# Linear attention and gated FFN in fp32 precision: product groups summed onto ScalarE's copies in PSUM, both parts of x in DRAM, and the first pass's outputs by Strassen's scheme

## The chip, the cores and the metric

The kernel runs on one core of one Trainium2 chip. The metric is the device time of one execution in microseconds (us); the median of several runs is given. One more execution was recorded by the hardware profiler, and every statement on single instructions comes from it. Engines: PE is TensorE's matmuls and PEld its weight loads, DVE is VectorE, ACT is ScalarE, POOL is GpSimd, SP is SyncE, which issues most of the DMAs.

## The reference

```python
def _attn_ref(q, k, v, w_phi):                       # q, k, v: 8 x 8 heads x 576 x 64
    def phi(x):
        proj = np.einsum('bhsd,df->bhsf', x, w_phi)  # 128 features
        proj = proj - np.max(np.abs(proj), axis=-1, keepdims=True)
        return np.concatenate([np.exp(proj), np.exp(-proj)], axis=-1)
    q_p, k_p = (phi(q), phi(k))
    kv = np.einsum('bhsf,bhsd->bhfd', k_p, v)
    z = np.sum(k_p, axis=2)
    num = np.einsum('bhsf,bhfd->bhsd', q_p, kv)
    den = np.einsum('bhsf,bhf->bhs', q_p, z)[..., None] + 1e-06
    return num / den

def _moe_ref(x, w_gate, w_val, w_out):               # x: 4608 tokens x 512, d_ff = 1536
    gate = 1.0 / (1.0 + np.exp(-(x @ w_gate)))
    val = x @ w_val
    return gate * val @ w_out
```

The result of the attention, with its heads side by side, is the x of the FFN. All is in fp32.

## The kernel before

**Precision.** A product of two fp32 matrices is made of three matmuls. Each operand is split into a high part, rounded to the type that TensorE multiplies at full speed (`fp32r`), and a low part, which is the rest. A product is high x high + high x low + low x high. The high part is a copy on ScalarE (CAST), the low part a subtraction on VectorE.

**Layout.** Features or hidden units lie on the 128 partitions and tokens along a row; `out` is 512 x 4608, feature by token. The hidden layer has 12 blocks of 128 units.

**Phase A** (about the first 600 us) does the attention in 32 steps (8 batches x 4 pairs of heads, `attend`), which write x to `xscr` in DRAM. Between these steps it does the first four hidden blocks of the FFN for chunks of 512 tokens: `load_x` (L900) brings a chunk of x and splits it, L925 multiplies gate and value, L982 the outputs, and the sum of the four blocks goes to `yscr` in DRAM (L1011).

**Phase B** does the other eight blocks, in four pairs of blocks, by Strassen's scheme: a product of 2 x 2 blocks is made of 7 products of combined blocks, not 8. One such product is called a *group* here (`group`). Its inputs are the seven weight combinations of a pair (made by `combine` from gate, value or output weights, each in a high and a low part) and seven blocks of x named 11, 21, 22, T1 to T4 (made by `x_blocks`). A group has 7 products; each is 6 matmuls of 128 x 384 (two steps of depth by three parts). In L1286 each product gets a PSUM bank, and VectorE adds the banks up (L1305) into buffers in SBUF, after ScalarE has copied the first one there (L1311): one copy and five additions a group. The results are four quarters: two feature halves by two halves of 384 tokens.

Phase B goes twice over the six chunks of 768 tokens, which are called turns here:

- In the *first pass* (`first_pass`), `x_blocks` loads four blocks of x, combines and splits all seven (ScalarE L1213, VectorE L1217), and stores T1 to T4 in `tscr`. Then come four groups (gate and value of pairs 0 and 1). The hidden halves are split, and the outputs are ordinary matmuls (L1407, 96 a turn). `finish` loads what phase A left in `yscr` (L1161), adds it (L1168) and writes `out` (L1172). Beside it, one combination of weights for the second pass is made in each turn.
- In the *second pass*, T1 to T4 come from `tscr`, the blocks 11, 21 and 22 from `xscr` and are split again. Four groups (pairs 2 and 3) are followed by two groups for the outputs (`sent`), each over both pairs. Their results are copied or added into SBUF and added to `out` by DMAs that GpSimd issues (L1516, accumulating). The last turn adds `out` itself, before it writes it.

**What sets the order.** Nothing is issued in the order of the source. Each operation is recorded with its engine, an assumed duration, what it reads and writes and a rank; `Plan.run` then walks through time and takes for each engine, of what could start within a short window (`NEAR`), the operation of lowest rank. For DMAs it assumes one wire with a rate (`RATE`) and a landing time. Buffers come from rings, which may share memory (`arena`, `r_f`, `r_y`, ...): whoever takes a slot waits for its last user. Each engine executes its list strictly in the order found so.

Of the kernel before, what the change touches and what calls it, by code (L numbers as in the profile page):

```python
# [20 lines left out]
P = 128  # L21
# [18 lines left out]
RB = 70 << 10  # L40
FB = 15 << 10
# [18 lines left out]
KEEP = 30.0  # L60
SPAN = 46.0
PASS = 43.8

# [87 lines left out]
class Plan:  # L151
# [5 lines left out]
    RATE = 0.26, 0.36  # L157

# [22 lines left out]
    def run(self):  # L181
        free = dict.fromkeys(self.NEAR, 0.0)
        ready = {e: [] for e in free}
        mode, wire, rate = None, 0.0, self.RATE[0]
# [30 lines left out]
        while left:  # L215
            best = None
            for e, cs in ready.items():
                ts = [(t, o) for o in cs if (t := start(o)) is not None]
                if not ts:
                    continue  # L220
                first = min(t for t, _ in ts) + self.NEAR[e]
# [18 lines left out]
            if o.eng in ("SP", "POOL"):  # L240
                wire = max(wire, t) + o.lag / rate * 1e-6
                end = wire + 2.0
# [4 lines left out]
            if o.opens:  # L247
                rate = self.RATE[1]
# [23 lines left out]
def attention_moe(  # L272
# [54 lines left out]
    for hd in range(2):  # L327
# [4 lines left out]
    xscr = [dram.tile([P, NC4, CW], F32, tag=f"xs{c}", name=f"xs{c}") for c in range(NCH)]  # L332
    yscr = [dram.tile([P, NC4, CW], F32, tag=f"ys{c}", name=f"ys{c}") for c in range(NCH)]
    tscr = [dram.tile([8, P, DC], F32, tag=f"t{c}", name=f"t{c}") for c in range(NDC)]
    wscr = [dram.tile([2, P, DM], F32, tag=f"wo{j}", name=f"wo{j}") for j in range(JA + 4)]
# [3 lines left out]
        for m in range(3)  # L339
    }  # L340
# [6 lines left out]
    third = arena("three", "third", FB, F32R)  # L347
# [12 lines left out]
    r_y1 = x.ring(3, DM)  # L360
    r_h = x.ring(8, 2 * HT)
    r_wo = x.ring(8, DM)
    r_hA = low(48).ring(4, 4 * HT)
    r_hB = low(42).ring(1, 3 * HT) + third().ring(3, 3 * HT)
    r_O = low(72).ring(2, 7 * 2 * P)
    x = high()
    r_G = x.ring(8, 7 * 2 * P)
    r_stage = x.ring(2, 7 * 2 * P)
    r_O += r_stage
    r_swo = high(56).ring(7, DM)  # L370
    r_x7 = high(42).ring(2 * NC4, CW)
    r_f = flat().ring(5, HT) + flat(12).ring(6, HT)
    r_tmp = flat(21).ring(3, 2 * HT)
    r_f2 = r_f[:5] + flat(8).ring(2, HT) + r_f[8:10]
    r_T = flat(12).ring(1, 3 * HT)
    r_V = flat(19.5).ring(2, 4 * HT)
    x = more()
    r_raw2, r_top2 = x.ring(2, 2 * DM, U32), x.ring(1, DM, U32)
    r_sum = x.ring(1, 2 * DM)
# [15 lines left out]
    def dve(n, fn, reads, writes, rank, k=1.0, after=()):  # L395
        return plan.op("DVE", 0.07 + n / 960 / k, 0.16, fn, reads, writes, rank, after=after)
# [18 lines left out]
    xmark = [Buf() for _ in range(NCH)]  # L415
    ymark = [Buf() for _ in range(NCH)]
    closing, opening, feeding, exps = [], [], [], []

    def attend(i):
# [346 lines left out]
        if b == 0:  # L766
# [9 lines left out]
            )  # L776
        t = 0
        while t < S:
# [4 lines left out]
                lambda c=c, o=o, t=t, wd=wd: nc.sync.dma_start(  # L783
                    xscr[c][:, p, o : o + wd], xp()[:, t : t + wd]
# [109 lines left out]
    def load_x(c, r, rings, after=()):  # L894
        for p in range(NP):
# [4 lines left out]
                lambda p=p, xl=xl: nc.sync.dma_start(xl().bitcast(F32), xscr[c % NCH][:, p, :]),  # L900
# [12 lines left out]
            )  # L913

# [71 lines left out]
    def first_js(c, r, step):  # L986
# [5 lines left out]
        for t in range(NC4):  # L992
            acc, y = Buf(banks, [P, CW]), Buf([r_y], [P, CW])

            def go(t=t, acc=acc):
# [15 lines left out]
                256 << 10, lambda t=t, y=y: nc.sync.dma_start(yscr[c][:, t, :], y()),  # L1011
# [39 lines left out]
    last.opens = [a().cells for a in (high, more)]  # L1051
# [15 lines left out]
    def combine(n, m, r, rings, after):  # L1067
# [7 lines left out]
        for i, j in enumerate(pair(n)):  # L1075
# [4 lines left out]
            dve(  # L1080
# [6 lines left out]
            )  # L1087
        p12, p21 = (1, 2) if m < 2 else (2, 1)
# [24 lines left out]
        combined.append(plan.ops[-1])  # L1113
# [24 lines left out]
    def out_weight(j, r, rings, after):  # L1138
        wh, wl = Buf(rings, [P, DM]), Buf(rings, [P, DM])
        weigh(j, 2, r, False, wh, wl, slice(0, DM), None, after, True)  # L1140
        return wh, wl

    def pieces(dc, h):

        t, e, s = dc * DC + h * HT, dc * DC + h * HT + HT, 0
        while t < e:
            c, o = divmod(t, CW)
            wd = min(CW - o, e - t)
            yield c, o, s, wd
            t, s = t + wd, s + wd  # L1150

    def final(m, dc, h):
        return out[m * P : m * P + P, dc * DC + h * HT : dc * DC + h * HT + HT]

    def finish(m, dc, h, acc, r):

        y1, y = Buf([r_y1], [P, HT]), Buf([r_y, r_f], [P, HT])
        for c, o, s, wd in pieces(dc, h):
            sp(
                wd << 9,  # L1160
                lambda c=c, o=o, s=s, wd=wd: nc.sync.dma_start(  # L1161
                    y1().bitcast(F32)[:, s : s + wd], yscr[c][:, m, o : o + wd]
                ),
                [(ymark[c], m)], [(y1, s)], r - 12.0, [done],
            )
        sums.append(dve(
            HT,
            lambda: vec.tensor_tensor(y(), acc()[:, :HT], y1().bitcast(F32), op=ALU.add),  # L1168
            [acc, y1], [y], -90.0,
        ))  # L1170
        sp(
            192 << 10, lambda: nc.sync.dma_start(final(m, dc, h), y()), [y],  # L1172
            [(omark[dc], (m, h))], r,
        )

    prior, taken, outs, sums = [fed], [], [], []
# [3 lines left out]
    def x_blocks(dc, r, again):  # L1180

        at_ = {n: (Buf([r_X], [P, 2, HT]), Buf([r_X], [P, 2, HT])) for n in XB}
        tmp = [] if again else [Buf([r_tmp], [P, 2, HT]) for _ in range(3)]
        n_, since = [0.0], len(plan.ops)
# [5 lines left out]
        def fetch(x, K, h):  # L1190
            for c, o, s, wd in pieces(dc, h):
                sp(
                    wd << 10,
                    lambda c=c, o=o, s=s, wd=wd: nc.sync.dma_start(
                        x().bitcast(F32)[:, :, s : s + wd],
                        xscr[c][:, 2 * K : 2 * K + 2, o : o + wd],
                    ),
                    [xmark[c]], [(x, s)], rank(), prior[-1:],
                )
# [10 lines left out]
        def split(n, src):  # L1210
# [9 lines left out]
                [src, xh] if src is not xl else [xh], [xl], rank(),  # L1220
            )
            if n in kinds and dc < NDC - 1:
                for i, x in enumerate(at_[n]):
                    k = 2 * kinds.index(n) + i
                    sp(
                        384 << 10, lambda k=k, x=x: nc.sync.dma_start(kept_x(k), flat_x(x)),
                        [x], [(tmark[dc], k)], r + 8.0,
                    )

# [6 lines left out]
        if again:  # L1236
            for n in XB:
                if n in kinds:
                    for i, x in enumerate(at_[n]):
                        k = 2 * kinds.index(n) + i  # L1240
                        sp(
                            384 << 10,
                            lambda k=k, x=x: nc.sync.dma_start(flat_x(x), kept_x(k)),
                            [(tmark[dc], k)], [x], rank(), prior[-1:],
                        )
                else:
                    fetch(at_[n][1], int(n[0]) - 1, int(n[1]) - 1)
                    split(n, at_[n][1])
            prior.append(plan.op("X", 0.0, 0.0, lambda: None, after=plan.ops[since:]))
            return at_  # L1250

        b11, b21, b22 = (at_[n][1] for n in ("11", "21", "22"))
        fetch(b11, 0, 0)
        fetch(tmp[0], 0, 1)
        fetch(b22, 1, 1)
        fetch(b21, 1, 0)
        less(tmp[1], tmp[0], b11)
        split("11", b11)
# [377 lines left out]
```

## Time and profile before

| | |
|---|---|
| median of 3 runs | 1170.73 us (1164.34 to 1174.84) |
| profiled execution | 1172.34 us, span 1170.5 us |
| mean granted TensorE clock | 0.997 |
| busy: PE, DVE, ACT, POOL | 1142.5, 951.3, 585.6, 39.2 us |
| DMA | 193.55 MB, mean 165 GB/s |

A row of a group of instructions reads: line, engine, operation, output tile <- input tiles, sizes, how many; then busy time and mean ns of one, the idle time of the engine just before them, and what ended most of it. A matmul's ns count from its issue to its end, and matmuls overlap: how fast they follow one another is seen in a window (busy time by the number of instructions). In a table of windows the columns after the engines are granted clock, mean busy share of the 16 DMA engines and GB/s.

### The profile page before, as it was taken

To read this page: it belongs to the slowest core of one execution; us is meant where nothing else is said; L and a number is where in the kernel's file an instruction comes from. 1 tells how busy PE (TensorE), PEld (TensorE's weight loads), DVE (VectorE), ACT (ScalarE), POOL (GpSimd) and SP (SyncE) were. 2 spreads that over 40 slices of the span, in tenths; PEclk is the share of its full clock that TensorE was granted. 3 is DMA by queue.
4 is the path that set the end of the run, shared out by engine and by line. 5 is a ranking of instruction groups with operands and counts; after the bars stand their busy time and mean duration, and the time that the engine had idled before them with its cause. 6 is when DMAs were issued, how large, how long until landed. Compare 5 with 4: busy or idle time off the path is not lost.

```text
span 1170.5 us, 22971 instructions
## 1 busy us (share of the span) xinstructions
PE 1142.5 (98%) x9012; PEld 966.3 (83%) x9012; DVE 951.3 (81%) x1826; ACT 585.6 (50%) x1095; POOL 39.2 (3%) x50
## 2 busy tenths in 40 slices
PE   8999989999999999999999999999999999999997
PEld 6666656767676767777879999999999999999997
DVE  6999898788888878847998898988987666867766
ACT  6767866666666666625554342452432323333331
POOL 0000000000000000000000000000000022021021
PEclk9999999999999999999999999999999999999999
DMA  6763554434435352226565747668397747547542
GB/s 234 213 211 108 151 168 119 136 121 126 145 79 164 104 171 86 79 81 205 172 233 199 254 157 286 208 215 296 106 344 275 246 70 171 164 55 181 171 55 54
DMA packets 110037, 193.55 MB, mean 165 GB/s; under 512 B 20200, under 2 KB 63336, under 8 KB 109928
## 3 DMA queue, kind: packets, MB, share of 16 engines
q1 hardware_dynamic: 103592, 183.42, 47.7%
q0 software_dynamic: 6336, 8.65, 5.7%
q8 instruction: 71, 1.16, 0.4%
q14 instruction: 38, 0.31, 0.1%
HBM read 125.17 MB, written 66.72 MB: 164 GB/s over the span
## 4 chain that ended last, share of the span: by engine, by line
PE 47%; issue 19%; DVE 16%; DMA 9%; ACT 4%; POOL 3%; SPq 1%; DVEq 0%; POOLq 0%; ACTq 0%
PE bank L1286 15%; PE gate L925 11%; PE gate L1407 4%; PE bank L632 4%; PE bank L674 3%; POOL out L1516 3%; PE gate L982 2%; DMA low<-ys 2%; DMA rb<-den 2%; DMA more<-w_moe 2%; PE bank L443 2%; PE bank L692 1%; DMA low<-xs 1%; PE bank L646 1%; DVE d L598 1%
## 5 line engine op out<-in xcount | busy, mean ns | idle before, releaser
L1286 PE MATMUL bank<-low,high 128*128 128x384 f32 x1785 | 326.9, 338 | 8.8 <-DVE flat L1305 6.6
L1286 PEld LDWEIGHTS bank<-low,high 128*128 128x128 f32 x1785 | 311.3, 189 | 13.0 <-issue 4.3
L1305 DVE TENSOR_TENSOR flat<-flat,bank 128x384 f32<-128x384 f32 x241 | 131.6, 549 | 64.0 <-PE bank L1286 51.3
L925 PE MATMUL gate<-low 128*128 128x512 f32 x696 | 165.7, 394 | 1.2 <-ACT flat L960 0.6
L925 PEld LDWEIGHTS gate<-low 128*128 128x128 f32 x696 | 128.6, 188 | 29.8 <-issue 1.2
L490 ACT ACTIVATE ek<-ek 128x512 f32<-128x512 f32 (+1 forms) x192 | 96.4, 527 | 27.1 <-DVE ek L478 25.7
L1407 PE MATMUL gate<-low 128*128 128x384 f32 x576 | 102.5, 335 | 0.0
L1407 PEld LDWEIGHTS gate<-low 128*128 128x128 f32 x576 | 100.3, 188 | 0.3 <-DVE flat L1168 0.3
L982 PE MATMUL gate<-low 128*128 128x512 f32 x384 | 92.3, 394 | 0.0
L982 PEld LDWEIGHTS gate<-low 128*128 128x128 f32 x384 | 70.8, 188 | 15.1 <-issue 1.0
L632 PE MATMUL bank<-ek,vin 128*32 128x256 f32 x1240 | 74.8, 387 | 4.8 <-ACT d L556 3.4
L632 PEld LDWEIGHTS bank<-ek,vin 128*32 128x32 f32 x1240 | 37.9, 111 | 47.0 <-issue 10.9
L1516 POOL DMA_DIRECT2D out<-flat x44 | 38.5, 950 | 1121.8 <-DVE flat L1305 994.2
L1286 PE MATMUL gate<-low,high 128*128 128x384 f32 x375 | 74.7, 336 | 0.8 <-ACT flat L1311 0.8
L1286 PEld LDWEIGHTS gate<-low,high 128*128 128x128 f32 x375 | 65.8, 188 | 1.1 <-ACT flat L1311 1.1
L449 DVE TENSOR_REDUCE mk<-bank 128x4 f32<-128x512 f32 (+1 forms) x92 | 48.8, 552 | 21.0 <-PE bank L443 18.1
L1311 ACT COPY flat<-bank 128x384 f32<-128x384 f32 x47 | 22.3, 475 | 66.7 <-PE bank L1286 66.2
L1305 DVE TENSOR_TENSOR flat<-flat,gate 128x384 f32<-128x384 f32 x59 | 32.4, 552 | 22.5 <-PE gate L1286 17.1
L478 DVE TENSOR_TENSOR ek<-bank,mk 128x512 f32<-128x512 f32 (+1 forms) x92 | 48.1, 550 | 0.4
L949 ACT CAST low<-flat 128x512 fp32r<-128x512 f32 x36 | 22.3, 620 | 47.2 <-DVE flat L974 43.6
L601 ACT ACTIVATE eq<-d 128x1152 f32<-128x1152 f32 x29 | 33.9, 1168 | 20.1 <-DVE d L598 19.7
L443 PE MATMUL bank<-wk,kin 64*128 64x128 f32 x496 | 38.7, 289 | 4.9 <-DMA kin<-k 4.4
(207 smaller groups left out, 1908.8 us busy)
## 6 DMA issues: line engine op xcount, KB each, us to landing
t<-low SPq DMA_DIRECT2D x40, 384.0 KB
low<-t SPq DMA_DIRECT2D x40, 384.0 KB
more<-w_moe SPq DMA_DIRECT2D x24, 512.0 KB
low<-xs SPq DMA_DIRECT2D x44, 256.0 KB
g<-high SPq DMA_DIRECT2D x12, 896.0 KB
kin<-k SPq DMA_DIRECT2D x32, 320.0 KB
qin<-q SPq DMA_DIRECT2D x32, 320.0 KB
vin<-v SPq DMA_DIRECT2D x32, 320.0 KB
```

The lines of the kernel that those rows point to most:

```text
L443: nc.tensor.matmul(pk[hd]()[:, t, :], x()[head(hd), t * P : t * P + P], wk[head(hd), :], start=True, stop=True,)
L449: vec.tensor_reduce(mx, pk, axis=AX.X, op=ALU.max, apply_absolute_value=True)
L478: vec.tensor_tensor(ek[g]()[:, :, F:], src, mk[g]()[:, :ns].unsqueeze(2).broadcast_to([P, ns, F]), op=ALU.subtract,)
L490: lambda g=g, sg=sg: act.activation(ek[g]()[:, :, sg * F : sg * F + F], ek[g]()[:, :, F:], AF.Exp, scale=1.0 - 2.0 * sg,),
L632: nc.tensor.matmul(o_[o : o + Q, : 2 * F], vx()[:, 2 * t + hd, o % D : o % D + Q], (e0, e1)[hd][:, t, :] if t < 4 else e2[:, 0, :], start= ...
L674: nc.tensor.matmul(nm()[o : o + Q, :], w()[:, sg, o : o + Q], es[sg]()[:, o // D, cs], start=sg == 0, stop=sg == 1, tile_position=(0, o),)
L925: nc.tensor.matmul(o(), a()[:, ws], x(), start=cc + n == 0, stop=cc == NC4 - 1 and n == 2,)
L982: nc.tensor.matmul(acc(), w()[:, ms], a(), start=first and i == 0, stop=last and i == 2)
L1286: nc.tensor.matmul(o()[:, :HT], s()[:, ws], y(), start=first and n + cc + i_ == 0, stop=end, skip_group_check=not first,)
L1305: lambda: vec.tensor_tensor(o(), p(), q()[:, :HT], op=ALU.add),
L1407: nc.tensor.matmul(acc()[:, :HT], w()[:, m * P : m * P + P], s()[:, h, :], start=i + e + k_ == 0, stop=i + e + k_ == 4,)
L1516: lambda f=f, h=h, t=t: nc.gpsimd.dma_start(final(f, dc, h), t(), accum_op=ALU.add),
```

## The change

1. **Groups in PSUM.** In `group` the running sums stay in PSUM. ScalarE copies a bank into the next product's bank (`seed`, L1298 of the new kernel, two in a group: a to b, b to c), and that product's matmuls (L1283) add to what they find there. A third copy (L1311) brings product d to SBUF as `q`, and VectorE adds it to two banks (L1304): two additions a group in place of five.
2. **Outputs by groups in both passes.** The first pass has no ordinary output matmuls. `sent` makes a group for each pair of blocks and each half of the features (7 products of 3 matmuls). In all turns but the last, its results are put in a buffer of 128 x 768 (ScalarE L1432, VectorE L1304), and GpSimd issues a DMA that adds it to `out` (L1437): 88 of 384 KB in place of 44 of 192 KB. Phase A's `y` goes straight to `out` (L1031); `yscr`, `finish` and the stored output weights are gone. The last turn makes both pairs in one group, as before.
3. **Both parts of x kept.** `keep_x` (L427) stores both parts of each piece of x in `xparts`, 72 stores of 256 KB in phase A. `x_blocks` loads the parts of the blocks 11, 21 and 22 (L1186) and splits only T1 to T4 in the first pass.
4. **Around it.** The hidden halves are combined and split one by one in `values`, in the first pass too. Output weights are combined in Strassen's form for all four pairs. Arena sizes, rings and some constants of the planner change (`KEEP`, `LAND`, `ACTN`).

In counts, before and after: groups 60 and 94; matmuls of 384 columns in phase B 3096 and 3024; VectorE's additions in groups 300 and 188; ScalarE's copies in groups 60 and 282.

On TensorE, a value group in the first pass, before. Names are the output bank, the arenas that hold weights and x, and the engine waited for:

```order
L1286 MATMUL bank_199<-low,high 128x384 x6
L1286 MATMUL bank_177<-low,high 128x384 [waits DVE_49]
L1286 MATMUL bank_177<-low,high 128x384 x5
L1286 MATMUL bank_175<-low,high 128x384 [waits DVE_49]
L1286 MATMUL bank_175<-low,high 128x384 x5
L1286 MATMUL bank_187<-low,high 128x384 [waits Activation_49]
L1286 MATMUL bank_187<-low,high 128x384 x5
L1286 MATMUL bank_177<-low,high 128x384 [waits DVE_49]
L1286 MATMUL bank_177<-low,high 128x384 x5
```

A product of six matmuls waits for VectorE (or ScalarE) to have emptied its bank. After, TensorE in groups of the first pass:

```order
L1283 MATMUL bank_162<-low,high 128x384 [waits DVE_49]
L1283 MATMUL bank_162<-low,high 128x384 x5
L1283 MATMUL bank_164<-low,high 128x384 x6
L1283 MATMUL bank_150<-low,high 128x384 x6
L1283 MATMUL gate_183<-low,high 128x384 [waits Activation_49]
L1283 MATMUL gate_183<-low,high 128x384 x5
L1283 MATMUL bank_164<-low,high 128x384 x6
L1283 MATMUL bank_152<-low,high 128x384 [waits Activation_49]
L1283 MATMUL bank_152<-low,high 128x384 x5
L1283 MATMUL gate_183<-low,high 128x384 x6
```

Products that add to a carried sum wait for ScalarE's copy into their bank, and products of two groups alternate. ScalarE in a first-pass turn, before:

```order
L1361 ACTIVATE flat<-flat 128x384 [waits DVE_49]
L1361 ACTIVATE flat<-bank_175 128x384 [waits DMAHW3_49,PE_49]
L1361 ACTIVATE flat<-flat 128x384 [waits DVE_49] x2
L1311 COPY flat<-bank_177 128x384 [waits DMAHW2_49,PE_49]
L1378 CAST low<-flat 128x384 [waits DVE_49] x2
L1311 COPY flat<-bank_187 128x384 [waits DMAHW3_49,PE_49]
L1378 CAST low<-flat 128x384 [waits DVE_49] x2
```

L1361 is the sigmoid, L1378 a hidden half's high part. ScalarE after, around the output groups of a first-pass turn (DMASW is an accumulating DMA that has to land):

```order
L1432 COPY flat<-gate_183 128x384
L1432 COPY flat<-bank_162 128x384 [waits PE_49]
L1432 COPY flat<-bank_164 128x384 [waits DMASW3_49]
L1382 CAST low<-flat 128x384 [waits DVE_49]
L1298 COPY gate_183<-bank_150 128x384 [waits PE_49,Activation_49]
L1298 COPY bank_162<-gate_176 128x384 [waits PE_49,Activation_49]
L1311 COPY flat<-bank_152 128x384 [waits PE_49]
L1311 COPY flat<-bank_164 128x384 [waits PE_49]
L1298 COPY bank_174<-gate_183 128x384 [waits DVE_49,PE_49]
L1298 COPY bank_152<-bank_162 128x384 [waits PE_49,Activation_49]
```

The carried copies (L1298) now stand behind output copies (L1432), some of which wait for an earlier accumulate.

The diff, cut to its core:

```diff
+    LAND = 2.0, 3.0
...
+    def keep_x(c, p, bufs, r):
+        for n, x in enumerate(bufs):
+            sp(
+                256 << 10,
+                lambda n=n, x=x: nc.sync.dma_start(
+                    xparts[n, :, p, c * CW : c * CW + CW], x().bitcast(F32)
+                ),
+                [x], [(pmark[c], (p, n))], r,
+            )
...
             sp(
-                256 << 10, lambda t=t, y=y: nc.sync.dma_start(yscr[c][:, t, :], y()),
+                256 << 10, lambda t=t, y=y: nc.sync.dma_start(
+                    out[t * P : t * P + P, c * CW : c * CW + CW], y()
+                ),
                 [y], [(ymark[c], t)], r,
             )
...
+        def parts(n):
+            for i, x in enumerate(at_[n]):
+                fetch(x, xparts[i], pmark, int(n[0]) - 1, int(n[1]) - 1)
...
-        less(tmp[1], tmp[0], b11)
-        split("11", b11)
+            less(t1, b12, b11)
+            parts("11")
+            split("T1", t1)
...
-        product(a, 0, "11", "11", True, False)
-        on_act(HT, lambda: act.copy(t1(), a()[:, :HT]), [a], [t1], -200.0)
-        product(b, 1, "S2", "T2", True, True)
-        add(t1, t1, b)
-        product(c, 2, "S3", "T3", True, False)
-        add(t2, t1, c)
...
-        product(d, 3, "S1", "T1", True, False)
-        add(t2, t2, d)
-        product(a, 4, "12", "21", False, True)
-        product(c, 5, "22", "T4", False, True)
-        add(t3, first, c)
-        product(d, 6, "S4", "22", False, True)
-        add(t1, t1, d)
-        return a, t2, t3, t1
+        def seed(o, src):
+            return on_act(
+                HT, lambda: act.copy(o()[:, :HT], src()[:, :HT]), [src], [o], -200.0, before
+            )
+        def add(o, p):
+            at_, y, part = o
+            dve(
+                HT, lambda: vec.tensor_tensor(at_(), p()[:, :HT], q(), op=ALU.add),
+                [p, q], [(y, part)], -200.0,
+            )
+        product(a, 0, "11", "11", True)
+        seed(b, a)
+        product(d, 1, "S1", "T1", True)
+        on_act(HT, lambda: act.copy(q(), d()[:, :HT]), [d], [q], -200.0)
+        product(b, 2, "S2", "T2", False)
+        opened = seed(c, b)
+        product(a, 3, "12", "21", False)
+        product(c, 4, "S3", "T3", False)
+        add(t2, c)
+        product(b, 5, "S4", "22", False)
+        add(t1, b)
+        product(c, 6, "22", "T4", False)
+        taken.append(opened)
+        return a, t2[1], c, t1[1]
...
+    def sent(sources, dc, m, r, banks, last):
+        ys = [Buf([wide], [P, 2, HT]) for _ in range(2)]
+        a, _, c, _ = group(
+            on_h(sources, m), r, banks, [(half(y, 1), y, 1) for y in ys], m == 1
+        )
+        for i, (y, src) in enumerate(zip(ys, (a, c))):
+            f = 2 * i + m
+            if not last:
+                on_act(
+                    HT, lambda y=y, src=src: act.copy(y()[:, 0, :], src()[:, :HT]),
+                    [src], [(y, 0)], -90.0,
+                )
+                plan.op(
+                    "POOL", 0.9, 384 << 10,
+                    lambda f=f, y=y: nc.gpsimd.dma_start(
+                        final(f, dc), flat_y(y), accum_op=ALU.add
+                    ),
+                    [y], [(omark[dc], f), *((ymark[c_], f) for c_ in under(dc))], r,
+                )
+                continue
...
+        pieces = [(ws[p, 2], h) for p, h in zip(pairs, hs)]
+        for i, sources in enumerate([pieces] if final_ else [[x_] for x_ in pieces]):
+            for m in range(2):
+                sent(sources, dc, m, r + 29.2 + 7.3 * (m if final_ else i), banks, final_)
```

More of the change, by code (lines that the diff above doesn't have):

```diff
@@ L220, in run @@
                     continue
-                first = min(t for t, _ in ts) + self.NEAR[e]
+                first = min(t for t, _ in ts) + (ACTN if late and e == 'ACT' else self.NEAR[e])
                 def key(x):
@@ L1050, in attention_moe @@
     last = plan.op("X", 0.0, 0.0, swap, after=closing)
-    last.opens = [a().cells for a in (high, more)]
+    last.opens = [a().cells for a in (high, more, staged)]
     for cells in (*last.opens, third().cells):
@@ L1112, in combine @@
             )
-        combined.append(plan.ops[-1])
+        combined.append(opened)
         return gh, gl
@@ L1136, in fetched, with under, final @@
         return out
[L1138 to L1176, printed above, removed]
+    def under(dc, h=None):
+        t, n = (dc * DC, DC) if h is None else (dc * DC + h * HT, HT)
+        return range(t // CW, (t + n - 1) // CW + 1)
+    def final(f, dc):
+        return out[f * P : f * P + P, dc * DC : dc * DC + DC]
+    prior, taken = [fed], []
     omark, tmark = ([Buf() for _ in range(NDC)] for _ in range(2))
@@ L1182, in x_blocks @@
         at_ = {n: (Buf([r_X], [P, 2, HT]), Buf([r_X], [P, 2, HT])) for n in XB}
-        tmp = [] if again else [Buf([r_tmp], [P, 2, HT]) for _ in range(3)]
-        n_, since = [0.0], len(plan.ops)
+        n_, since, stores = [0.0], len(plan.ops), []
         def rank():
@@ L1269, in x_blocks, with group, product, go @@
+        prior.append(
+            plan.op(
+                "X", 0.0, 0.0, lambda: None, after=[o for o in plan.ops[since:] if o not in stores]
+            )
+        )
         return at_
-    def group(terms, r, banks, temps, names=names[0], plus=None):
+    def group(part, r, banks, sums=None, ahead=False):
         a, b, c, d = (Buf(banks, [P, CW]) for _ in range(4))
-        t1, t2, t3 = (Buf([temps], [P, HT]) for _ in range(3))
-        def product(o, i, w, xn, first, last):
-            k = names.index(w) * KH
-            for n, (weight, part) in enumerate(terms):
-                def go(weight=weight, part=part, n=n):
-                    cs, xs_ = part(k, xn)
+        q, *sums_ = (Buf([temps], [P, HT]) for _ in range(1 if sums else 3))
+        t1, t2 = sums or ((y, y, None) for y in sums_)
+        before = taken[-2:-1] if ahead else taken[-2:]
+        def product(o, i, w, xn, first):
+            terms = part(w, xn)
+            for n, (weight, steps, bufs, ks) in enumerate(terms):
+                def go(n=n, weight=weight, steps=steps, ks=ks):
@@ new lines, in sent @@
+                    [(y, h)], [(omark[dc], (f, h))], r,
+                )
+    ws, marks = {}, {}
+    for n in range(2):
+        for m in range(2):
+            ws[n, m] = combine(n, m, base - 30.0 + 20.0 * n + 10.0 * m, [r_G], [])
+    for n in range(2):
+        ws[n, 2] = combine(n, 2, base + 10.0 + 10.0 * n, [r_O], [])
+    start = base + 150.0
+    makes = [None, (2, 0), (2, 1), (3, 0), (3, 1), (2, 2)]
+    turns = [*range(NDC), NDC - 1, *range(NDC - 1)]
+    temps, hrings, wide, wait = r_f, r_h, r_w, [done]
```

515 lines of the change are left out of this document (210 added, 305 removed).

## The prediction

> **What bounds the kernel now.** I read the page first: its span, the busy shares, the chain by engine.
>
> ```profile
> span 1170.5 us, 22971 instructions
> PE 1142.5 (98%) x9012; PEld 966.3 (83%) x9012; DVE 951.3 (81%) x1826; ACT 585.6 (50%) x1095; POOL 39.2 (3%) x50
> PE 47%; issue 19%; DVE 16%; DMA 9%; ACT 4%; POOL 3%; SPq 1%; DVEq 0%; POOLq 0%; ACTq 0%
> ```
>
> TensorE is busy for 98% and heads the chain, so an edit is worth what it takes from TensorE's instructions or from the 28 us in which TensorE stands. Next I read the busy time by stage, and one stretch of the second pass.
>
> ```profile
> core 0: us, PE busy (x) PEld busy (x) DVE busy (x) ACT busy (x) POOL busy (x), PEclk, DMA share, GB/s
> 0.00:600.00 600.00, 587.05 (x5867) 419.43 (x5868) 499.84 (x1021) 379.94 (x739) 0.69 (x6) 1.00 0.47 145
> 600.00:930.00 330.00, 323.11 (x1826) 318.02 (x1825) 279.37 (x525) 129.26 (x240) 0.00 (x0) 0.99 0.68 236
> 930.00:1170.00 240.00, 232.38 (x1323) 228.84 (x1321) 172.12 (x282) 76.37 (x116) 38.48 (x44) 1.00 0.52 119
> ...
> 930.00:960.00 30.00, 30.00 (x174) 29.94 (x173) 20.74 (x37) 8.79 (x14) 7.15 (x8) 1.00 0.55 107
> ```
>
> Where nothing is late, 174 matmuls take 30.00 us: 0.1724 us for one of 384 columns. At that price the 1323 of the last stretch need 228.1 of 240 us, and the 1826 of the middle one 314.8 of 330 (a little more, since some are wider). So phase B, the Strassen part, loses at most 27 us. What TensorE stands for I read from the matmul line of the groups (released by, us in total, times):
>
> ```profile
> DVE flat L1305: 8.9, 10
> issue: 4.3, 4
> ACT flat L1311: 3.7, 6
> DVE low L1217: 3.4, 2
> DVE low L1474: 3.0, 2
> ACT high L1104: 2.7, 2
> ```
>
> No wait dominates, and 15.3 of these 26 us end with VectorE. The groups of instructions give the prices:
>
> ```profile
> L1286 PE MATMUL bank<-low,high 128*128 128x384 f32 x1785 | 326.9, 338 | 8.8 <-DVE flat L1305 6.6
> L1305 DVE TENSOR_TENSOR flat<-flat,bank 128x384 f32<-128x384 f32 x241 | 131.6, 549 | 64.0 <-PE bank L1286 51.3
> L1407 PE MATMUL gate<-low 128*128 128x384 f32 x576 | 102.5, 335 | 0.0
> L1311 ACT COPY flat<-bank 128x384 f32<-128x384 f32 x47 | 22.3, 475 | 66.7 <-PE bank L1286 66.2
> L1217 DVE TENSOR_TENSOR low<-low 128x768 fp32r<-128x768 f32 x33 | 31.0, 951 | 5.0 <-ACT low L1213 5.0
> L1213 ACT CAST low<-low 128x768 fp32r<-128x768 f32 x33 | 27.6, 836 | 29.8 <-DMA low<-xs 27.7 <-PE bank L1286 1.0 <-PE gate L1286 1.0
> L1168 DVE TENSOR_TENSOR flat<-gate,low 128x384 f32<-128x384 f32 x48 | 26.4, 552 | 10.8 <-DMA low<-ys 8.5 <-PE gate L1407 2.2
> L1516 POOL DMA_DIRECT2D out<-flat x44 | 38.5, 950 | 1121.8 <-DVE flat L1305 994.2
> ```
>
> **TensorE's own work.** L1407 is 576 matmuls: 96 for each of six turns of the first pass, after 24 products of 7 multiplied in groups. Four output groups replace them with 4 x 7 x 3 = 84. That is 12 less in a turn and 72 in all, as the order has it (3096 to 3024). By the clean stretch it is 72 x 0.1724 = 12.4 us; by L1407's own 102.5 / 576 = 0.178 it is 12.8. It comes straight off the path. I take -12.4.
>
> **VectorE's work.** A group has two additions in place of five: 60 x 5 = 300 become 94 x 2 = 188, 112 x 0.549 = 61.5 us less. The 33 splits of L1217 go (31.4), and the 48 additions of L1168 (26.5). Against it stand 14 more operations in each of the six first-pass turns (seven combinations of the hidden blocks for two pairs, where four plain halves were enough: 84 x 0.55 = 46 us), some 10 us for splits that were wide and are now narrow in the second pass, and some 7 us of weight combinations ahead of phase B. Net about -56 of 951. Most of that comes in the second pass. In a first-pass turn it is -6.6 - 2.9 - 4.4 for additions, splits and L1168, +4.4 for the output groups' additions and +7.7: about -2 of some 38 us (0.85 of a turn of 264 x 0.1724, by the middle window). So I don't let all of VectorE's waits go. L1217's 3.4 us go with its instructions, now loads. Of L1305's and L1474's 11.9 I let 4 go: L1305 now feeds a buffer at the end of a group and no running sum that a bank waits for. But ScalarE's 3.7 and 2.7 don't go, and some of the rest moves to the new order. That is -7.4. The last turn, which has no work of a following turn to put between, gets narrower splits and pays for L1474's half of it again, by some 2 us. I take -5 (between 0, all replaced, and -15.3, all of VectorE's).
>
> **Copies in PSUM.** Two copies a group now carry a partial sum from one bank to another, 188 in all; no row shows a copy into PSUM. The nearest is L1311's, 475 ns into SBUF. TensorE needs the copied bank six, nine or more matmuls after the source is complete. Six, the case of 87 of the 188 in the order, is 6 x 0.172 = 1.03 us, with the next product's first instruction 1.2 us. The need is 0.34 us for the last matmul (L1286's 338 ns), 0.475 for the copy and about 0.1 of handovers: 0.91. Hence nothing is lost where ScalarE is free, and something where it is in another instruction (L1311's 0.475 to L1213's 0.836 us). ScalarE goes up by (282 - 60) copies and 88 - 11 for outputs, 299 x 0.475 = 142, less L1213's 27.6: about 115, to 60% of the span. If one tight copy in five is late by 0.3 us, it is 87 / 5 x 0.3 = 5 us; if none, 0. I take +3, and 14 as the far end.
>
> The page "PSUM — Partial Sum Buffer" of the Trainium skill (Specifications) says that ScalarE writes to PSUM faster than to SBUF. By it a carried copy would undercut 475 ns and this term would be nearer 0; no row of before shows such a copy.
>
> **Accumulating DMAs.** These I read from the queues, the issues and two stretches of 5 us:
>
> ```profile
> q1 hardware_dynamic: 103592, 183.42, 47.7%
> q0 software_dynamic: 6336, 8.65, 5.7%
> out<-flat POOLq DMA_DIRECT2D x44, 192.0 KB, 4.4
> ...
> 865.00:870.00 5.00, 5.00 (x31) 5.00 (x30) 4.87 (x12) 1.93 (x5) 0.00 (x0) 1.00 1.03 426
> 945.00:950.00 5.00, 5.00 (x30) 5.00 (x30) 1.68 (x4) 0.96 (x2) 3.38 (x4) 1.00 1.04 136
> ```
>
> q0 is the 44 accumulates of L1516: 5.7% of 1170.5 us is 66.7 us of all 16 engines, 1.52 us for 192 KB. In the two stretches all engines are full, once with plain transfers (426 GB/s), once with accumulates (136). Before, all of these ran in the second pass. Now there are 88 of 384 KB, 48 of them in the first, 8 a turn. One costs 1.52 us if the price goes by rows (their number stays 128, each twice as long) and 3.03 if by bytes; I take 2.0, nearer the first. The buffers (seven of 384 KB, on memory that the groups' temporaries and the gates use too) come free when the accumulate has landed, and the order gives 39 to 63 matmuls, 6.7 to 10.9 us, from the data to TensorE's need. One lands 4.4 us after its issue, 2.9 more than its 1.52 of transfer, so a bunch of four takes 2.9 + 4 x 1.52 = 9.0 to 2.9 + 4 x 3.03 = 15.0 us, and 10.9 at 2.0. The shortfall is 0 where TensorE's need comes late, and 15.0 - 10.9 = 4.1 us a turn, 25 in the pass, at the far price. ScalarE stands at its copy into such a buffer (L1432 of after), with the carried copies of the next group behind it, and TensorE waits for those. A small case is in the trace:
>
> ```profile
> DVE flat L1305 <- DMA out<-flat: 11.9, 8, 2.0
> ACT flat L1504 <- DMA out<-flat: 6.0, 1, 6.0
> ```
>
> TensorE lost nothing by that 6.0 us (it lies in the clean stretch). I take +4 (0.7 us a turn, for the tight ones of a bunch); 0 is the lower end, since nothing here can help, and 25 the upper, without queueing of plain traffic. In the second pass at least 234 matmuls, 40 us, are left, and it costs nothing there.
>
> The page "DMA: Bandwidth & Descriptors" (SWDGE anatomy) of the Trainium skill prices such a DMA at about 2.0 us and its bytes at 436 GB/s. That is an estimate of 2.45 us for 192 KB, which the trace contradicts with 4.4; by it 384 KB would land in 2.9 us and this term would be 0.
>
> **Phase A and the rest.** 72 stores of 256 KB keep both parts of x: 18.9 MB. At q1's 558 us for 183.42 MB that is 57 us of the engines in about 500, on a share of 0.47. They wait on SyncE's queue for ScalarE's and VectorE's parts, ahead of later loads. I take 0, hidden by free DMA time, and 3 us either way if not. Loading parts rather than splitting takes no more than the lead of 20 us that the first pass plans.
>
> **Sum.** Against the profiled run's 1172.34 us (1.8 outside the span): -12.4 - 5 + 3 + 4 = -10.4, 1161.9. The median of the runs, 1170.73, is 1.6 lower: 1160.3, so 1160.
>
> **Rivals.** *A: DMA paces the first pass; slower.* A first-pass turn moves ten blocks of x and eight stores of 384 KB, two raw weights of 512 KB and two combined ones of 896: 9.96 MB. At the 426 GB/s stretch's 1.03 share that is 24 us; at the middle window's 0.68 share for 236 GB/s it is 2.88 us a MB, 29 us. With 8 accumulates at 1.52 to 3.03 (12 to 24 us) it is 36 to 53 us, and TensorE's turn is 252 x 0.1724 = 43.4. For it: the middle, 26 + 16 = 42, is already full. Against it: before has a share of only 0.68 there, with about as many plain bytes. It decides from 2.2 us an accumulate, where 26 + 17.6 reaches the turn. At the far end it is 10 us x 6 = 60 more; halfway, with stalls for buffers, 3 to 7 us a turn, 18 to 42: 1178 to 1202. *The rule that speaks for it stands on the same page ("Issuing engines are not separate DMA queues" of "DMA: Bandwidth & Descriptors", the Trainium skill): what POOL and SyncE issue interleaves on the same 16 engines. The 945 to 950 stretch agrees, with a share of 1.04 at 136 GB/s.*
>
> *B: ScalarE paces the groups; no change.* Carried copies queue behind sigmoids, hidden-part casts and output copies. If each of 87 tight ones loses 0.15 to 0.25 us, and accumulates cost 4, it is 13 to 22 in place of 3: 1170 to 1179. Against it: ScalarE is under 40% in the middle stage and goes to about 60.
>
> *C: almost no wait stays; faster.* If VectorE's 15.3 us go, and neither copies nor accumulates cost anything, it is 1172.3 - 12.4 - 15.3 - 1.6 = 1143. The clean 30 us with 69% of VectorE speak for it; the 85% of the first pass, hardly less now, against it.
>
> *D: the products don't fall by 72*, because the last turn or a transition adds some; the order rules it out.
>
> **How the numbers follow.** The forecast (1150 to 1169) has 0.46, A 0.27, B 0.13, C 0.13, the rest 0.01. One per cent, 11.7 us, is about what a measurement of this kernel can tell; faster is below 1159.0, slower above 1182.4. The forecast lies across the first bound, 0.26 below and 0.20 above; C is faster; B is no change, and 0.03 of A. Faster 0.40, no change 0.35, slower 0.25 (0.24 of A, 0.01 of the rest). The range leaves out C's lower edge and A's far end: 1145 to 1198.
>
> **What would show it.** Right: 3024 matmuls of 384 columns in the Strassen part at about 0.172 us; no idle before them ended by the x splits; carried copies near 475 ns with under 5 us of TensorE's idle ended by them; ScalarE's waits on accumulates of the first pass present, and TensorE's idle behind them under 8 us. Wrong: DMA share near 1 through 600 to 870 us with x loads or accumulates ahead of TensorE's idle (A); ScalarE above 70% with tens of short waits for its copies (B); idle in phase B under 8 us (C). A longer phase A, by more than 3 us, would break the term that I put at nothing.

## The result, and the profile after

The changed kernel takes 1206.91 us (median of 4 runs, 1205.61 to 1210.14) against 1170.39 for the kernel before (4 runs): a ratio of 1.032, 95% interval 1.0269 to 1.0371. It is 36.5 us slower, where 10 us faster was forecast. The profiled execution takes 1206.62 us with a span of 1204.7.

The page of the changed kernel, the lines that answer to those of before:

```profile
span 1204.7 us, 23398 instructions
PE 1146.8 (95%) x8940; PEld 959.9 (80%) x8940; DVE 893.5 (74%) x1801; ACT 713.7 (59%) x1465; POOL 77.9 (6%) x94
q1 hardware_dynamic: 103080, 197.18, 48.0%
q0 software_dynamic: 12672, 34.61, 16.2%
out<-flat POOLq DMA_DIRECT2D x48, 384.0 KB, 9.0
out<-third POOLq DMA_DIRECT2D x40, 384.0 KB, 7.1
```

The work is what was forecast: 72 matmuls less, VectorE down by 58 us, ScalarE up by 128 (115 forecast). TensorE stands for 58 us in place of 28. The same kernel by stage (columns as before: engines, granted clock, DMA share, GB/s), with two cuts of 10 us:

```profile
0.00:600.00 600.00, 588.89 (x5868) 418.79 (x5869) 498.73 (x1024) 378.51 (x742) 0.70 (x6) 0.99 0.54 174
600.00:955.00 355.00, 312.24 (x1661) 296.10 (x1662) 261.37 (x511) 200.14 (x430) 42.16 (x48) 0.96 0.81 237
955.00:1180.00 225.00, 224.97 (x1296) 224.65 (x1295) 118.72 (x239) 127.53 (x280) 35.05 (x40) 1.00 0.74 193
...
670.00:680.00 10.00, 3.57 (x12) 3.57 (x13) 0.00 (x0) 0.49 (x1) 0.00 (x0) 0.53 1.06 319
690.00:700.00 10.00, 10.00 (x58) 9.68 (x57) 9.67 (x21) 7.33 (x16) 0.00 (x0) 1.00 0.21 62
```

Phase A costs nothing (5868 matmul records in 600 us, 5867 before). The second pass is free of gaps: 1296 matmuls in 225 us are 0.1736 us each. The loss lies in the first pass. Its 1661 matmuls would need 286 us at 0.1724 and have 355; some 69 us go there. The stretch from 600 to 930 us of the kernel before lost 15.

What TensorE stood for before the groups' matmuls (L1283), by what ended it (us, times), and then who waited for an accumulating DMA to land (us in total, times, longest). The first list, like all lists of this kind here and in the prediction, adds up the idle time of PE and that of its weight loads (PEld), which stand for much the same stretches. So it shows what TensorE waited for, but here more than twice the time:

```profile
DVE flat L1304: 36.4, 36
DMA low<-xparts: 24.3, 7
ACT bank L1298: 17.4, 11
ACT gate L1298: 15.4, 8
...
DVE flat L1304 <- DMA out<-flat: 24.4, 11, 5.9
ACT flat L1364 <- DMA out<-flat: 22.3, 9, 4.6
ACT flat L1432 <- DMA out<-flat: 9.2, 7, 4.2
```

VectorE and ScalarE wait 56 us for buffers that an accumulate still holds: at the groups' additions, at the sigmoids (L1364) and at the output copies. What stands behind these on the same engine is late for TensorE: L1304's additions, which empty banks, and L1298's carried copies. Counted on PE alone, the idle time before L1283 is 42 us: 16.7 end with L1304, 13.3 with the carried copies and 11.8, over a quarter, with a load of x's parts. In each turn the accumulates, the stores of T1 to T4 and the loads of x for the next turn fall together (DMA share 1.06 from 670 to 680 us), with a quiet stretch behind them (0.21 from 690 to 700).

### The profile page after: what moved, and what is told of

Read it like the earlier page. It is cut to its first block, busy times and chain, and to the rows that moved or that the text cites. A ratio compares the mean times of both kernels' runs of the same rounds, so it can differ in the third digit from the quotient of the medians.

```text
span 1204.7 us, 23398 instructions
## 1 busy us (share of the span) xinstructions
PE 1146.8 (95%) x8940; PEld 959.9 (80%) x8940; DVE 893.5 (74%) x1801; ACT 713.7 (59%) x1465; POOL 77.9 (6%) x94
## 3 DMA queue, kind: packets, MB, share of 16 engines
q1 hardware_dynamic: 103080, 197.18, 48.0%
q0 software_dynamic: 12672, 34.61, 16.2%
## 5 line engine op out<-in xcount | busy, mean ns | idle before, releaser
L1283 PE MATMUL bank<-low,high 128*128 128x384 f32 x1284 | 246.6, 342 | 9.6 <-ACT bank L1298 7.6
L1283 PEld LDWEIGHTS bank<-low,high 128*128 128x128 f32 x1284 | 227.3, 191 | 15.3 <-ACT bank L1298 9.4
L1283 PE MATMUL gate<-low,high 128*128 128x384 f32 x732 | 147.6, 344 | 16.7 <-DMA low<-xparts 10.8
L945 PEld LDWEIGHTS gate<-low 128*128 128x128 f32 x708 | 131.9, 191 | 37.9 <-issue 5.3
L1283 PEld LDWEIGHTS gate<-low,high 128*128 128x128 f32 x732 | 131.3, 193 | 19.8 <-DMA low<-xparts 11.4
L1437 POOL DMA_DIRECT2D out<-flat x48 | 42.2, 1033 | 891.8 <-DMA low<-xparts 648.2
L1283 PE MATMUL bank<-low 128*128 128x384 f32 x396 | 89.5, 343 | 10.3 <-DVE flat L1304 10.1
L1382 ACT CAST low<-flat 128x384 fp32r<-128x384 f32 x130 | 63.3, 513 | 32.9 <-DVE flat L1391 30.1
L1283 PEld LDWEIGHTS bank<-low 128*128 128x128 f32 x396 | 71.2, 191 | 13.0 <-DVE flat L1304 9.0
L1002 PEld LDWEIGHTS gate<-low 128*128 128x128 f32 x372 | 68.6, 188 | 14.5 <-issue 1.0
L1304 DVE TENSOR_TENSOR flat<-bank,flat 128x384 f32<-128x384 f32 x89 | 48.1, 550 | 33.5 <-DMA out<-flat 18.1
L1385 DVE TENSOR_TENSOR low<-flat,low 128x384 fp32r<-128x384 f32 x113 | 60.2, 549 | 11.5 <-ACT low L1382 11.5
L1304 DVE TENSOR_TENSOR flat<-gate,flat 128x384 f32<-128x384 f32 x55 | 30.2, 552 | 47.3 <-PE gate L1283 36.3
L1391 DVE TENSOR_TENSOR flat<-flat,bank 128x384 f32<-128x384 f32 x26 | 14.3, 550 | 52.9 <-PE bank L1283 48.8
L1283 PE MATMUL gate<-low 128*128 128x384 f32 x218 | 51.0, 340 | 2.5 <-DVE flat L1304 2.5
```

The source lines that it names most:

```text
L945: nc.tensor.matmul(o(), a()[:, ws], x(), start=cc + n == 0, stop=cc == NC4 - 1 and n == 2,)
L1002: nc.tensor.matmul(acc(), w()[:, ms], a(), start=first and i == 0, stop=last and i == 2)
L1283: nc.tensor.matmul(o()[:, :HT], s()[:, ws], y, start=first and n + cc + i_ == 0, stop=n == len(terms) - 1 and cc == steps - 1 and i_ == 2, ...
L1304: HT, lambda: vec.tensor_tensor(at_(), p()[:, :HT], q(), op=ALU.add),
L1382: on_act(HT, lambda: act.copy(hh(), y()), [y], [hh], -100.0, after)
L1385: lambda: vec.tensor_tensor(hl(), y(), hh().bitcast(F32), op=ALU.subtract),
```

## The experiments

All times are medians, each with runs of the kernel before beside it on the same chip (1167.7 to 1169.2 us); ratios are to those.

**e1_plain**: the first pass's output DMAs overwrite.

```diff
-                        final(f, dc), flat_y(y), accum_op=ALU.add
+                        final(f, dc), flat_y(y)          # first pass only
```

> The 48 output DMAs of the first pass overwrite instead of adding (same queue, same bytes, same order on every engine; what phase A and the first of the two pairs left in out is lost, so this part of the sum is left out). If the read-modify-write price (2.17 us of all 16 engines for 384 KB in the first pass, against about 1 us plain) paces the first pass, some 56 us of DMA time go from it, its DMA share falls from 0.81 to under 0.75, TensorE's idle there falls by more than half and the time is 1160 to 1180. If the loads of x's parts, the planner's order or the copies in PSUM are what costs, it stays above 1195.

1160.66 us, ratio 0.9931 (0.9906 to 0.9956). The order on each engine is that of the changed kernel, so the loss of 36.5 us, and 8.6 more, hangs on these 48 DMAs adding to `out` instead of overwriting it. The queue's row:

```profile
q0 software_dynamic: 9600, 34.61, 11.7%
out<-flat POOLq DMA_DIRECT2D x48, 384.0 KB, 5.2
```

In the changed kernel 88 accumulates take 16.2% of 1204.7 us, 195 us of all 16 engines, 2.22 each. Here q0 has 11.7% of 1161.7, 136 us; without 40 x 2.22 for the second pass, 47 are left, an estimate of 0.98 for a plain one. They land after 5.2 us, not 9.0.

**e2_tiny**: the same DMAs with 96 of 768 columns.

```diff
-                        final(f, dc), flat_y(y), accum_op=ALU.add
+                        final(f, dc)[:, :96], flat_y(y)[:, :96], accum_op=ALU.add   # first pass only
```

> The 48 output DMAs of the first pass move 96 of their 768 columns (an eighth of the bytes, so seven eighths of the first pass's outputs are left out); order unchanged. If the outputs' DMA is the whole cause, the first pass runs like the second (no idle beyond some us) and the time is 1148 to 1165. If a mere landing delay of about 2.5 us a slot were the cause, or the parts of x, it stays above 1180.

1156.00 us, ratio 0.9879 (0.9853 to 0.9906). TensorE's idle at L1283:

```profile
DVE flat L1304: 8.7, 24
ACT bank L1298: 1.9, 3
DVE low L1210: 1.8, 2
```

Without the accumulates' bytes, 13.2 us are gained. My sum without its term for them was -14.4. So the parts of x, the carried copies and VectorE's work cost together about what I had put down for them; the run doesn't tell them apart.

**e3_price**: one number of the planner.

```diff
-                    "POOL", 0.9, 384 << 10,
+                    "POOL", 0.9, 768 << 10,
```

> Only the planner's assumption changes: an accumulate takes 768 KB of its wire, 2.1 us, in place of 384 KB, 1.07 us, so that it is near what the trace shows (2.17). If the loss comes from an order that was made with too cheap accumulates (loads and buffers asked for too early), it falls to 1165 to 1190; if the engines' time itself is short, it stays at 1195 to 1215.

1176.07 us, ratio 1.0065 (1.0041 to 1.0089). The kernel does the same work and the same accumulates; only the order changes, and 30 of the 50 us between the changed kernel (+36.5 against before) and e2_tiny (-13.2) are gone. The waits for landing on VectorE are 2.7 us in place of 24.4, and those at the sigmoids and output copies are no longer listed. TensorE's idle now ends mostly with loads (on PE alone: x's parts 13.3 us, L1304 3.7):

```profile
DMA low<-xparts: 28.2, 10
DVE flat L1304: 11.7, 20
ACT bank L1298: 5.3, 8
...
DVE flat L1304 <- DMA out<-flat: 2.7, 5, 1.2
```

The three runs split the 50 us: 30 for an order that took an accumulate for 1.09 us (384 KB at the planner's rate of 0.36 MB a us) where it takes 2.2 (e3_price takes it for 2.18); 15 more for adding instead of overwriting (e3_price to e1_plain); 5 for the bytes (e1_plain to e2_tiny). e1_plain keeps the old order, so the second step may hold some of the first. The planner also takes 3.0 us for landing after the wire time, where 7.1 to 9.0 us pass from issue to landing; no run changes that.

**e10_rows**: each accumulate of the first pass issued as two halves.

```diff
-                        final(f, dc), flat_y(y), accum_op=ALU.add
+                        final(f, dc)[:, s:e], flat_y(y)[:, s:e], accum_op=ALU.add   # for (s, e) in (0, 384), (384, 768)
```

> The changed kernel, its order of engines untouched, with each of the 48 accumulates of the first pass issued as two of half the columns: the same bytes in twice the rows. If the price goes by rows (140 to 190 ns for a row of 1536 B before, 250 for one of 3072 B now), an accumulate takes 2.8 to 3.0 us in place of 2.2, and a first pass that hangs on it gets 20 to 45 us longer: 1225 to 1255. If it goes by bytes or the loss is not due to accumulates, 1203 to 1215.

1205.18 us, ratio 1.0321 (1.0298 to 1.0344). The queue's row:

```profile
q0 software_dynamic: 19584, 34.61, 17.3%
```

q0 takes 17.3% of 1202.6 us, 13 us more than in the changed kernel, 0.27 for each of the 48. So the price goes mostly by bytes. As the dose came out this small, the run doesn't show what more DMA time would cost.

**e5_not**: T1 to T4 made again in the second pass.

```diff
-            if dc < NDC - 1:                 # stores of T1 to T4
+            if False:
-        if again:                            # loads of T1 to T4
+        if False:
+    r_tmp2 = x.ring(3, 2 * HT)               # from the second pass's output buffers
...
```

> T1 to T4 are not stored and loaded again but made again in the second pass, from x (12 loads of 384 KB more, 8 fewer, per turn there; VectorE some 7.6 us and ScalarE 3.4 us more per second-pass turn, which have room at 53% and 57%). The first pass loses 40 stores of 384 KB, about 1 us of all engines each. If DMA time paces the first pass, it gets 25 to 40 us shorter and the time is 1168 to 1188; if only landing delay of the accumulates counts, it stays above 1198.

1243.43 us, ratio 1.0645 (1.0592 to 1.0697); a miss. A window of the first pass and one of the second:

```profile
600.00:955.00 355.00, 317.15 (x1689) 302.13 (x1688) 266.84 (x523) 204.28 (x441) 42.49 (x48) 0.96 0.71 196
955.00:1170.00 215.00, 191.21 (x1052) 189.88 (x1052) 121.00 (x221) 115.10 (x240) 28.08 (x32) 0.94 0.58 139
```

The first pass does 1689 matmuls in 355 us, 28 more than the changed kernel: 5 us for 40 stores. That speaks against plain DMA time as what held the first pass while the planner had the wrong price, although the order changed too. The second pass broke (1052 matmuls in 215 us, where a clean one does 1238). It had three buffers fewer for outputs, its x made later and more work on VectorE and ScalarE; which of these it was, I didn't try. The expectation also miscounted the loads: a second-pass turn has four more and eight fewer, not twelve more, and the SyncE queue moved 173.59 MB where the changed kernel moves 197.18.

**e6_tlate, e7_split and e8_both**, on top of e3_price: the stores of T1 to T4 later; the blocks 11, 21 and 22 split again in the first pass; both.

```diff
-                        [x], [(tmark[dc], k)], r + 8.0,
+                        [x], [(tmark[dc], k)], r + 8.0, (), 15.0,      # e6, e8
...
-            parts("11")
+            split("11", b11)                                           # e7, e8; 21 and 22 too
```

> On top of the corrected price (e3_price): the stores of T1 to T4 are planned 15 us after their data are ready, out of the burst in which x is loaded for the next turn and the outputs are accumulated, into the stretch with a DMA share of 0.2 to 0.8. If the burst is what is left of the loss (28 us of TensorE's idle end with a load of x's parts), the time is 1160 to 1171; if the mean DMA time is, it stays at 1174 to 1180.

> On top of the corrected price: the blocks 11, 21 and 22 are split again in the first pass (three splits a turn, 2.9 us of VectorE and 2.5 us of ScalarE), not loaded as parts: 36 loads of 384 KB, about 36 us of all DMA engines, leave the first pass. If DMA time in the burst is what is left of the loss, the time is 1160 to 1171; if VectorE or ScalarE is by now as near its limit as the DMA engines, 1174 to 1190.

> Corrected price, late stores of T1 to T4 and split blocks together. If the burst of DMA alone holds the first pass, nothing of it is left and the time is 1154 to 1164, below the kernel before by about 12.4 us of saved matmuls; if it stays above 1170, something beside the DMA engines (VectorE, ScalarE's copies) holds it.

1168.29 us (0.9967 to 1.0011), 1166.24 (0.9959 to 1.0004) and 1166.64 (0.9962 to 1.0001). Set against the kernel before beside each, e3_price is 6.9 us above it, e6_tlate 0.5 below and e7_split 2.5 below: each alone brings 7 to 9 us. The waits for x's parts fall from 28.2 to 10.2 us in e6_tlate (from 13.3 to 4.8 on PE alone) and are gone in e7_split. A window of the changed kernel, of e6_tlate and of e8_both, and e6_tlate's line for x's parts:

```profile
645.00:870.00 225.00, 197.20 (x1055) 187.49 (x1054) 171.42 (x330) 133.07 (x284) 30.92 (x36) 0.95 0.83 239
645.00:870.00 225.00, 212.10 (x1174) 203.48 (x1173) 189.72 (x367) 146.47 (x314) 36.17 (x40) 0.99 0.94 269
645.00:870.00 225.00, 211.34 (x1172) 202.97 (x1172) 204.83 (x390) 155.59 (x328) 35.51 (x40) 0.99 0.82 223
DMA low<-xparts: 10.2, 4
```

e6_tlate does 119 matmuls more than the changed kernel at a higher mean DMA share, 0.94, so it is not the mean share that held the changed kernel. The burst was a part of what e3_price had left, 7 of the 20 us between it and e2_tiny; for e7_split, which also moves fewer bytes, burst and bytes aren't told apart. Both together bring no more: 1166.64 lies between the two ranges of the expectation. TensorE's idle at L1283 in e8_both:

```profile
DVE flat L1304: 12.4, 19
ACT low L1127: 6.9, 2
ACT bank L1298: 6.7, 13
DVE low L1210: 5.4, 7
```

VectorE is busy for 204.83 of the 225 us from 645 to 870, 91%, but that doesn't show that it holds the first pass: e12_split1 below has 205.85 in the same stretch and does 1223 matmuls, and e11_halfsplit has 210.24 and does 1206, against 1172 here. What holds e8_both is not settled. The 6.9 us (3.3 on PE alone) are output weights that come late once, at 656 us.

**e9_half and e11_halfsplit**: on top of e6_tlate and e8_both, pair 0's outputs are stored plainly in five turns and added by VectorE in the second pass.

```diff
+            if keep:
+                sp(384 << 10, lambda ...: nc.sync.dma_start(y2[f, :, dc * DC : dc * DC + DC], flat_y(y)), ...)
+                continue
```

> On top of e6_tlate (corrected price, late stores of T1 to T4): in five of the six first-pass turns the outputs of pair 0 are stored plainly in a buffer of their own, and VectorE adds them in the second pass (loads of 384 KB and 8 additions of 0.55 us a turn there, where VectorE stands at 53%). 20 of the first pass's 48 accumulates become plain stores, about 1.2 us of all DMA engines less each, 24 us. If DMA time still holds the first pass of e6_tlate, it is 1156 to 1163; if VectorE (84% there) and the copies do, 1164 to 1170; if the additions and loads slow the second pass, above 1172.

> The same on top of e8_both, where the blocks 11, 21 and 22 are split and not loaded as parts (VectorE 91% busy, DMA share 0.79 in the first pass). If VectorE holds that kernel, the cheaper outputs bring nothing: 1163 to 1169. If accumulates still do, 1155 to 1162.

1171.56 us (1.0018 to 1.0059) and 1169.75 (1.0001 to 1.0032). Windows of e9_half, first and second pass:

```profile
645.00:870.00 225.00, 215.12 (x1192) 206.51 (x1191) 194.24 (x375) 148.31 (x321) 21.70 (x24) 0.99 0.87 277
915.00:1140.00 225.00, 222.25 (x1261) 217.90 (x1261) 133.93 (x275) 114.27 (x251) 34.96 (x40) 1.00 0.83 228
```

The first pass gains: 1192 matmuls against 1174 in e6_tlate, 3 us, and in e11_halfsplit 1206 against 1172 in e8_both, 6 us. That speaks for the accumulates still holding a part of both, although the order changed too. The second pass gives more back: 1261 against 1294 in e6_tlate, 6 us, and 1247 against 1297 in e8_both, 9 us; its idle in e9_half ends mostly with the groups' additions into the output buffers, which share VectorE with the new ones. Neither result lies in a range of its expectation (e9_half between two, e11_halfsplit 0.75 us above).

**b1_seeds**: the kernel before, with the new group alone.

```diff
-        add(t1, t1, b)
+        seed(b, a)
...
-        return a, t2, t3, t1
+        return a, t2, c, t1
```

> The kernel before with the new group alone: sums carried by ScalarE's copies in PSUM, two additions in place of five in its 60 groups; outputs, x blocks and DMAs as before. By my terms (waits -5, carried copies +3) it is 1163 to 1172; if ScalarE's copies pace the groups (87 tight ones at 0.15 to 0.25 us), 1178 to 1190; if nearly all of TensorE's 15 us of waits for VectorE go with it, 1152 to 1160.

1206.89 us, ratio 1.0326 (1.028 to 1.0373), above all three ranges. The edit also gives each output group one more copy on ScalarE. Its second pass stands at the hidden splits, which are still made in two wide pieces (again PE and PEld together; on PE alone 12.5, 6.8, 4.1 and 3.7 us):

```profile
ACT low L1466: 26.6, 10
DVE low L1471: 15.2, 11
DVE flat L1309: 12.3, 22
ACT bank L1305: 10.4, 15
```

The copies themselves (ACT bank L1305 here) are the smallest of these. So the new group doesn't do well by itself. In the changed kernel, where each hidden block is split by itself, the second pass is clean, which speaks for the narrow splits as its needed companion; that wasn't tried on the kernel before, and why its quarters come later for a wide split isn't settled.

**e12_split1**: e7_split, with turn 0 loading its parts.

```diff
-            split("11", b11)
+            split("11", b11) if dc else parts("11")                    # 21 and 22 too
```

> e7_split, but turn 0 loads the parts of 11, 21 and 22 (the DMA share around 600 us is 0.5 to 0.65, VectorE's share over 90%, and 7.4 us of TensorE's idle end with the output weights that VectorE makes late); turns 1 to 5 split. If those 7 us are VectorE's overload at the start alone, the time is 1157 to 1162, below both kernels. If the late weights come back in another place, it stays at 1164 to 1169.

1160.54 us, ratio 0.9932 (0.9905 to 0.9959): 0.7% below the kernel before, which is little but clear of the interval, and 46 us below the changed kernel. The late weights (7.4 us in e7_split's list, 3.5 on PE alone) don't come back, and the first pass does 1223 matmuls in 225 us:

```profile
645.00:870.00 225.00, 219.15 (x1223) 210.25 (x1222) 205.85 (x386) 158.13 (x338) 35.41 (x40) 1.00 0.83 235
915.00:1140.00 225.00, 225.00 (x1297) 224.84 (x1296) 118.52 (x240) 125.30 (x274) 34.95 (x40) 1.00 0.73 193
```

## Why the prediction was wrong

**TensorE's work, -12.4: right.** 8940 matmuls in place of 9012, and 0.1736 us each where nothing is late.

**VectorE's waits, -5, and carried copies, +3: right as a sum, not shown one by one.** In e2_tiny, where the accumulates are nearly away, the whole change is worth -13.2 against my -14.4. The -5 rests on a misread list: it adds PE and PEld, and on PE alone the waits at L1286 in the kernel before are 11.0 us, 9.6 of them ended by VectorE, not 15.3 of 26. By this count the bound of -15.3, and with it rival C, reached nearly 6 us too far; that the sum came out so near is in part luck. It also holds only for the change as a whole: the new group by itself cost the kernel before 38 us (b1_seeds). The copy into PSUM, which no row had shown, takes 466 ns, and the copy into SBUF in the same kernel 480:

```profile
L1298 ACT COPY bank<-bank 128x384 f32<-128x384 f32 x68 | 31.7, 466 | 23.8 <-PE bank L1283 21.2 <-DVE flat L1391 0.2
L1311 ACT COPY flat<-bank 128x384 f32<-128x384 f32 x68 | 32.6, 480 | 14.4 <-PE bank L1283 13.1
```

What the page "PSUM — Partial Sum Buffer" of the Trainium skill (Specifications) says of ScalarE, faster to PSUM than to SBUF, agrees, by 14 ns. Rival B falls with the second pass: ScalarE is busy for 57% there, with all its carried copies, and TensorE for 224.97 of 225 us; and in e2_tiny only 1.9 and 0.4 us of the idle list end with carried copies.

**Phase A, 0: right.** The DMA share rose from 0.47 to 0.54 and no matmul came later.

**Accumulating DMAs, +4: this is the step that failed. They cost about 50 us** (+36.5 against the kernel before, and -13.2 with an eighth of the first pass's output bytes). The price of one was nearly right, 2.22 us for my 2.0, and so was the landing: a median of 9.0 us in the first pass for a bunch that I gave 10.9. Wrong was what I set them against, and what I left out:

- I counted the matmuls from an output's data to *TensorE's* need of its buffer and took 6.7 to 10.9 us as the allowance. But the buffers share memory with the groups' temporaries and the gates, and those who waited were VectorE's additions and ScalarE's sigmoids, 47 of the 56 us of waits. Each wait holds up all that stands behind it on its engine. I had named that queue for L1432 only, which had 9.2 us of the waits, and then priced it at 0.7 us a turn.
- I set DMA time against a whole turn: 42 us of 43.4, "already full", as rival A. The measured mean was no limit: 0.83 from 645 to 870 us, where e6_tlate does 119 matmuls more at 0.94. The engines were full for 20 to 30 us of each turn and at 0.2 to 0.6 in other stretches. What decided was an order made with half the price (e3_price takes back 30 us with not a byte less) and, for a smaller part, the coincidence of accumulates, T stores and the next turn's loads (7 us in e6_tlate). I read the order but not the assumption about durations that it was made with, although the planner's rate and landing time stand in the code.
- I left out what idle TensorE time brings in its train. In the first pass of the changed kernel the granted clock was halved in six spells, 31 us together (670 to 680 us above has a mean of 0.53), in which 67 matmuls ran; at 0.1724 us extra each that is an estimate of 12 us, against 2 in the first pass before. e3_price has three such spells there, e12_split1 none (1.00). The page "TensorE: Matmul & The Clock Gate" of the Trainium skill (Part 1) ties half rate to an idle window of some 3.4 us. The traces agree on the length, each spell lasting 3.4 us or a multiple; the window ahead was not wholly idle here, TensorE stood for 61% to 92% of its 3.4 us.

**The rivals.** A had the right place, sign and nearly the size (1178 to 1202 "with stalls for buffers"), and I gave it 0.27. Its reason was half right: that the DMAs add is the cause (e1_plain), but they don't pace the pass by their mean load. My argument against it, the share of only 0.68 before, was an average over stretches that the change moved new work into unevenly. C, almost no wait left, is nearest to what e2_tiny shows, and would have needed outputs that cost nothing.

The estimate that I made from the page "DMA: Bandwidth & Descriptors" of the Trainium skill (SWDGE anatomy), 2.9 us to land, is too short by a factor of 2.4 to 3.1 here: 7.1 us in the second pass (DMA share 0.74), 9.0 in the first. Its other rule, that what different engines issue interleaves on the same 16 DMA engines, agrees: in e1_plain, where only GpSimd's DMAs changed, the waits for SyncE's loads of x's parts fall from 24.3 to 7.9 us.

## What to carry to other kernels

Before an order made by a planner is trusted, compare the duration that it assumes for a *new* kind of transfer with the trace: here one number, 1.09 us for 2.22, was worth 30 us. When a transfer holds a buffer that other engines' temporaries share, its landing time is to be set against every next user of that memory and the queue behind that user, not against the bottleneck engine alone. Weigh DMA load in the stretch in which the transfers fall, not over a turn, and ask whether plain stores whose readers are far off can move out of it.

## What was not expected of the hardware

An accumulating DMA of 384 KB takes 2.22 us of all 16 DMA engines, 2.3 times the plain one's 0.98 on the same queue (both worked out above from q0's shares); splitting its rows in two adds only 0.27 us. In the kernel before, 192 KB took 1.52, and the halves of e10_rows, 192 KB in the same layout, 1.25 each ((2.22 + 0.27) / 2); the difference is not explained by these runs.
